# Attention and a max-of-three FFN on one core: scores as stationary operand, per-partition normalization, paired heads, and an instruction order written by hand

## The chip, the cores and the metric

The kernel runs on one core of one Trainium2 chip. The metric is the device time of a whole execution in microseconds (us). A kernel's executions mostly agree within 1.5%; where one fell in a slower state it is left out of the medians and the ratios, and this is said. "Span" is the time from the first to the last instruction in the trace; the timed value of the same execution is some 2 us longer (261.6 against 259.6 us). Engines: PE is TensorE (PEld its weight loads), DVE VectorE, ACT ScalarE, POOL GpSimd, SP SyncE.

## The reference

```python
# q, k, v: (4 batches, 8 heads, 768 positions, 64), fp32; n_sink = 4, window = 64
rel    = pos[:, None] - pos[None, :]
causal = rel >= 0
keep   = causal & ((pos[None, :] < n_sink) | (rel < window))   # streaming heads
mask   = causal for heads with is_retrieval == 1, keep for the others
a   = softmax(where(mask, q @ k.T / 8, -1e9))
x   = (a @ v), heads side by side          # (3072 tokens, 512)
h   = maximum(maximum(x @ w1, x @ w2), x @ w3)      # d_ff = 768
out = h @ w_out                            # (3072, 512), fp32
```

Which heads are retrieval heads is data. So each kernel computes the whole causal triangle for all heads. Near the diagonal it multiplies the exponentials by a mask; for keys two blocks or more back it uses a copy of V scaled by the head's flag (`vf`; `va` is V with a column of ones, which yields the softmax sums).

## The kernel before

Both kernels work on pairs of heads, 16 pairs in all, four to a batch. The parts that the change touches:

```python
# loads: cast to fp16 by DMAs that POOL issues, one batch at a time
nc.gpsimd.dma_start(out=qn, in_=q[b].rearrange("h (sb p) d -> p h sb d", p=P))   # kn, vn alike
# prep of a pair: 24 transposes, one per head and block, for q and k; vf by VectorE
nc.tensor.transpose(tqv[hl*D:(hl+1)*D, sb*P:(sb+1)*P], qn[:, 2*hp+hl, sb, :], ident)
nc.vector.tensor_scalar(out=vf[:, 1:NSB, hl, 0:D+1], in0=va[:, 1:NSB, hl, 0:D+1],
                        scalar1=RT[:, h:h+1], scalar2=None, op0=ALU.mult)
# ... scores, exp, and a mask of 256 columns per head and key block on POOL ...
# value product: V is the stationary operand, the scores stream; out is [65, queries]
nc.tensor.matmul(op_t[0:D+1, a0:a1], lhs,                      # lhs: va or vf
                 pt[:, ki, a0-ki*P : a1-ki*P], start=..., stop=...)
nc.vector.tensor_copy(out=osg[0:D+1, 0:S], in_=op_t[0:D+1, 0:S])
nc.sync.dma_start(out=sdram[h:h+1, 0:S], in_=osg[D:D+1, 0:S])  # the sums go to DRAM
# ... at the batch's end, all eight heads:
nc.sync.dma_start(out=sums_b[0:H, 0:S], in_=sdram)
nc.vector.reciprocal(out=rcp[0:H, 0:S], in_=sums_b[0:H, 0:S])
nc.sync.dma_start(out=rdram, in_=rcp[0:H, 0:S])
for h in range(H):
    nc.sync.dma_start(out=bc[0:D, 0:S], in_=rdram[h:h+1, 0:S].to_broadcast([D, S]))
    nc.vector.tensor_tensor(out=xTb[hp][hb:hb+D, 0:S], in0=ostages[h][0:D, 0:S],
                            in1=bc[0:D, 0:S], op=ALU.mult)
# order: the FFN of batch b is written whole, after the attention of batch b+1
if pending_ffn is not None:
    ffn_batch(*pending_ffn)
pending_ffn = (xTb, b * S)
```

A scheduler then orders the instructions on each engine.

The softmax here doesn't subtract the row's maximum and nothing guards it: scores larger than these inputs give would overflow.

Of the kernel before, what the change touches and what calls it, by code (L numbers as in the profile page):

```python
# [9 lines left out]
FP16 = mybir.dt.float16  # L10
# [4 lines left out]
NEG = -30000.0  # L15


def _split_at(a, b, cut):
    out = []
    if a < min(b, cut):  # L20
        out.append((a, min(b, cut)))
    if max(a, cut) < b:
        out.append((max(a, cut), b))
    return out
# [3 lines left out]
def kernel(  # L28
# [14 lines left out]
    nc = tc.nc  # L43
# [6 lines left out]
    HD = H * D  # L50
    KS = HD // P
# [4 lines left out]

    assert D == 64, "kernel assumes head_dim == 64"
    assert S % P == 0 and HD % P == 0 and DF % P == 0 and NT % P == 0
    assert window <= P and n_sink <= P
    assert DMdl <= 512, "final matmul free dim must fit one PSUM bank"  # L60

    consts = ctx.enter_context(tc.tile_pool(name="consts", bufs=1))
    persist = ctx.enter_context(tc.tile_pool(name="persist", bufs=1))
    qkvp = ctx.enter_context(tc.tile_pool(name="qkvp", bufs=2))
    pairp = ctx.enter_context(tc.tile_pool(name="pairp", bufs=3))
    headp = ctx.enter_context(tc.tile_pool(name="headp", bufs=4))
    ostp = ctx.enter_context(tc.tile_pool(name="ostp", bufs=H + 2))
    bcp = ctx.enter_context(tc.tile_pool(name="bcp", bufs=2))
    bcp3 = ctx.enter_context(tc.tile_pool(name="bcp3", bufs=3))
    xtp = ctx.enter_context(tc.tile_pool(name="xtp", bufs=2))  # L70
    htp = ctx.enter_context(tc.tile_pool(name="htp", bufs=2))
    ptp = ctx.enter_context(tc.tile_pool(name="ptp", bufs=3))
    fwork = ctx.enter_context(tc.tile_pool(name="fwork", bufs=3))
    sps = ctx.enter_context(tc.tile_pool(name="sps", bufs=4, space=bass.MemoryType.PSUM))
    ops = ctx.enter_context(tc.tile_pool(name="ops", bufs=1, space=bass.MemoryType.PSUM))
    fsp = ctx.enter_context(tc.tile_pool(name="fsp", bufs=2, space=bass.MemoryType.PSUM))
    dramp = ctx.enter_context(tc.tile_pool(name="dramp", bufs=2, space=bass.MemoryType.DRAM))

    ident = consts.tile([P, P], FP16, name="ident")
    make_identity(nc, ident)  # L80

    tri = consts.tile([P, P], FP16, name="tri")
    nc.gpsimd.memset(tri, 0.0)
    nc.gpsimd.affine_select(
        out=tri, in_=tri, compare_op=ALU.is_ge, fill=NEG,
        base=0, pattern=[[1, P]], channel_multiplier=-1,
    )
    ediagn = consts.tile([P, P], FP16, name="ediagn")
    nc.gpsimd.memset(ediagn, 0.0)
    nc.gpsimd.affine_select(  # L90
        out=ediagn, in_=ediagn, compare_op=ALU.is_gt, fill=NEG,
        base=window, pattern=[[-1, P]], channel_multiplier=1,
    )
    ediag0 = consts.tile([P, P], FP16, name="ediag0")
    nc.vector.tensor_copy(out=ediag0, in_=ediagn)
    if n_sink > 0:
        nc.vector.memset(ediag0[0:n_sink, :], 0.0)
    esubn = consts.tile([P, P], FP16, name="esubn")
    nc.gpsimd.memset(esubn, 0.0)
    nc.gpsimd.affine_select(  # L100
        out=esubn, in_=esubn, compare_op=ALU.is_gt, fill=NEG,
        base=-window, pattern=[[-1, P]], channel_multiplier=1,
    )
    esub0 = consts.tile([P, P], FP16, name="esub0")
    nc.vector.tensor_copy(out=esub0, in_=esubn)
    if n_sink > 0:
        nc.vector.memset(esub0[0:n_sink, :], 0.0)
    tri01 = consts.tile([P, P], FP16, name="tri01")
    nc.gpsimd.memset(tri01, 1.0)
    nc.gpsimd.affine_select(  # L110
        out=tri01, in_=tri01, compare_op=ALU.is_ge, fill=0.0,
        base=0, pattern=[[1, P]], channel_multiplier=-1,
    )
    w01dn = consts.tile([P, P], FP16, name="w01dn")
    nc.vector.tensor_copy(out=w01dn, in_=tri01)
    nc.gpsimd.affine_select(
        out=w01dn, in_=w01dn, compare_op=ALU.is_gt, fill=0.0,
        base=window, pattern=[[-1, P]], channel_multiplier=1,
    )
    w01d0 = consts.tile([P, P], FP16, name="w01d0")  # L120
    nc.vector.tensor_copy(out=w01d0, in_=w01dn)
    if n_sink > 0:
        nc.vector.tensor_copy(out=w01d0[0:n_sink, :], in_=tri01[0:n_sink, :])
    w01sn = consts.tile([P, P], FP16, name="w01sn")
    nc.gpsimd.memset(w01sn, 1.0)
    nc.gpsimd.affine_select(
        out=w01sn, in_=w01sn, compare_op=ALU.is_gt, fill=0.0,
        base=-window, pattern=[[-1, P]], channel_multiplier=1,
    )
    w01s0 = consts.tile([P, P], FP16, name="w01s0")  # L130
    nc.vector.tensor_copy(out=w01s0, in_=w01sn)
    if n_sink > 0:
        nc.vector.memset(w01s0[0:n_sink, :], 1.0)
    cause01 = consts.tile([P, 2 * P], FP16, name="cause01")
    nc.vector.tensor_copy(out=cause01[:, 0:P], in_=tri01)
    nc.vector.memset(cause01[:, P : 2 * P], 1.0)
    wmc_n = consts.tile([P, 2 * P], FP16, name="wmc_n")
    nc.vector.tensor_copy(out=wmc_n[:, 0:P], in_=w01dn)
    nc.vector.tensor_copy(out=wmc_n[:, P : 2 * P], in_=w01sn)
    nc.vector.tensor_tensor(out=wmc_n, in0=wmc_n, in1=cause01, op=ALU.subtract)  # L140
    wmc_0 = consts.tile([P, 2 * P], FP16, name="wmc_0")
    nc.vector.tensor_copy(out=wmc_0[:, 0:P], in_=w01d0)
    nc.vector.tensor_copy(out=wmc_0[:, P : 2 * P], in_=w01s0)
    nc.vector.tensor_tensor(out=wmc_0, in0=wmc_0, in1=cause01, op=ALU.subtract)
# [5 lines left out]
    )  # L150
    retr_row = consts.tile([P, H], FP32, name="retr_row")
# [3 lines left out]
    RB = consts.tile([P, H], FP32, name="RB")  # L155
    nc.vector.tensor_scalar(
        out=RB[:, 0:H], in0=RT[:, 0:H], scalar1=-1.0, scalar2=1.0,
        op0=ALU.mult, op1=ALU.add,
    )
    sinkcol = consts.tile([P, 1], FP32, name="sinkcol")  # L160
    nc.vector.memset(sinkcol, 0.0)
    if n_sink > 0:
        nc.vector.memset(sinkcol[0:n_sink, :], 1.0)
    rowfac = consts.tile([P, H], FP32, name="rowfac")
    for h in range(H):
        nc.vector.tensor_tensor(
            out=rowfac[:, h : h + 1], in0=RT[:, h : h + 1],
            in1=sinkcol[:, 0:1], op=ALU.max,
        )

    w_t = [persist.tile([P, KS, DF], FP16, name=f"w{wi}t") for wi in range(3)]
    woutt = persist.tile([P, NNB, DMdl], FP16, name="woutt")
# [8 lines left out]
    TBW = next(w for w in (384, 512, 256, 128) if S % w == 0)  # L181

    def ffn_batch(xTb, t_glob):
        hTb = [htp.tile([P, S], FP16, tag=f"hT{i}", name=f"hT{i}") for i in range(NNB)]
        for tb0 in range(0, S, TBW):
            for ni in range(NNB):
                acc = fwork.tile([P, TBW], FP32, tag="facc")
                for wi, wt in enumerate(w_t):
                    yy = fsp.tile([P, 512], FP32, tag="fsp", name="yy")
                    for ks_i in range(KS):  # L190
                        nc.tensor.matmul(  # L191
                            yy[:, 0:TBW],
                            wt[:, ks_i, ni * P : (ni + 1) * P],
                            xTb[ks_i][:, tb0 : tb0 + TBW],
                            start=(ks_i == 0), stop=(ks_i == KS - 1),
                        )
                    if wi == 0:
                        nc.scalar.copy(out=acc, in_=yy[:, 0:TBW])  # L198
                    elif wi == 1:
                        nc.vector.tensor_tensor(  # L200
                            out=acc, in0=acc, in1=yy[:, 0:TBW], op=ALU.max
                        )
                    else:
                        nc.vector.tensor_tensor(  # L204
                            out=hTb[ni][:, tb0 : tb0 + TBW],
                            in0=acc, in1=yy[:, 0:TBW], op=ALU.max,
                        )
        for tb0 in range(0, S, P):
            yo = fsp.tile([P, 512], FP32, tag="fsp", name="yo")
            for ns in range(NNB):  # L210
                nc.tensor.matmul(  # L211
                    yo[:, 0:DMdl],
                    hTb[ns][:, tb0 : tb0 + P],
                    woutt[:, ns, 0:DMdl],
                    start=(ns == 0), stop=(ns == NNB - 1),
                )
            ot = fwork.tile([P, DMdl], FP32, tag="ot")
            nc.scalar.copy(out=ot, in_=yo[:, 0:DMdl])
            nc.sync.dma_start(out=out[t_glob + tb0 : t_glob + tb0 + P, :], in_=ot)
# [199 lines left out]
```

## Time and profile before

| | before |
|---|---|
| time, median of 4 runs beside the changed kernel | 359.1 us |
| span of the profiled run | 355.8 us |
| start / attention alone / attention and FFN / FFN alone | 27 / 85 / 205 / 39 us |

The first lines of the profile's page give busy time, share of the span and instructions of each engine:

```profile
PE 281.7 (79%) x1776; PEld 152.1 (43%) x1776; DVE 228.8 (64%) x417; ACT 131.4 (37%) x329; POOL 163.2 (46%) x226
```

PE's 79% looks like a bound, but the durations of its matmuls overlap; the prediction works out from spacings that its work is about 198 us. The timeline of VectorE at the end of the first batch's attention (start, us, line, operation, count) shows why the FFN starts late:

```profile
88.24 4.93 DVE L364 RECIPROCAL rcp<-sums_b 8x768 f32<-8x768 f32 x1
...
103.07 0.94 DVE L373 TENSOR_TENSOR xT<-osg,bc 64x768 f16<-64x768 f32 x1
103.94 5.39 DVE L269 TENSOR_SCALAR vf<-va,RT 128x325 f16<-128x325 f16 x1
104.58 4.75 DVE L358 COPY osg<-op_t 65x768 f32<-65x768 f32 x1
```

The sums are there at 88 us. Between the reciprocal and the first product lie 10 us, with a store, a broadcast load and preparation of other pairs; after it VectorE stands 5 us in a `vf` and an `osg` whose normal durations are 0.3 and 0.95 us. The first FFN matmul is at 112.2 us.

### The profile page before, as it was taken

The page shows a single profiled execution, that of the slowest core. Times are in us where ns is not written, and L with a number is a line of the kernel's source. Part 1 is how long each engine was busy: PE and PEld are TensorE (multiplying, and loading weights), DVE is VectorE, ACT ScalarE, POOL GpSimd, SP SyncE. Part 2 cuts the span into 40 slices and gives each one's busy share as a digit, 9 for nine tenths or more (in the row PEclk, how much of TensorE's full clock was granted, in tenths as well). Part 3 has the DMA queues.
Part 4 walks back from the last instruction along what each step waited for, and adds up shares of the span by engine and source line. Part 5 has one row for each costly group of instructions (what it writes and reads, how often), then busy time and mean ns, then how long its engine had stood idle before and what let it go on. Part 6 is the DMA issues. An engine that isn't in the chain of part 4 may idle for free.

```text
span 355.8 us, 4977 instructions
## 1 busy us (share of the span) xinstructions
PE 281.7 (79%) x1776; PEld 152.1 (43%) x1776; DVE 228.8 (64%) x417; ACT 131.4 (37%) x329; POOL 163.2 (46%) x226
## 2 busy tenths in 40 slices
PE   0028698668886869997998896979979859899995
PEld 0013365344455435553544453435445534445542
DVE  2715475479789988999935877983454485915530
ACT  1006426605642613426255420704756311132223
POOL 3550999949978952527327700731557400000000
PEclk9999999955576978999999998989999996999999
DMA  0999999999999990032040001201300003240004
GB/s 0 79 150 192 199 91 89 85 69 77 93 135 130 136 88 6 0 92 92 21 158 1 3 3 57 102 22 59 120 2 3 1 5 92 88 177 2 0 5 173
DMA packets 82522, 25.78 MB, mean 72 GB/s; under 512 B 74978, under 2 KB 77282, under 8 KB 82498
## 3 DMA queue, kind: packets, MB, share of 16 engines
q0 software_dynamic: 76288, 12.58, 50.9%
q1 hardware_dynamic: 6210, 12.88, 11.0%
q8 instruction: 14, 0.23, 0.3%
q14 instruction: 10, 0.08, 0.1%
HBM read 31.56 MB, written 6.49 MB: 107 GB/s over the span
## 4 chain that ended last, share of the span: by engine, by line
PE 35%; DVE 15%; POOL 9%; issue 5%; ACT 2%; DMA 1%; POOLq 0%; DVEq 0%; ACTq 0%
PE yy L191 19%; POOL pt L322 9%; PE yo L211 8%; DVE xT L373 4%; PE op_t L349 4%; PE st L307 2%; DVE acc L200 2%; DVE osg L358 2%; ACT pt L315 2%; DVE rcp L364 2%; DVE hT L204 1%; DVE vf L269 1%; DMA bc<-rdram 1%; DVE va L264 1%; DVE dm_n L278 1%
## 5 line engine op out<-in xcount | busy, mean ns | idle before, releaser
L315 ACT ACTIVATE pt<-st 128x512 f16<-128x512 f32 (+3 forms) x256 | 94.9, 473 | 105.5 <-PE st L307 99.4
L322 POOL TENSOR_TENSOR pt<-pt,dm_n 128x256 f16<-128x256 f16 (+1 forms) x160 | 106.3, 695 | 21.6 <-DVE va L267 11.0
L307 PE MATMUL st<-QT,KT 64*128 64x512 f16 (+3 forms) x256 | 56.5, 348 | 15.1 <-ACT pt L315 9.3
L322 POOL TENSOR_TENSOR pt<-pt,dm 128x256 f16<-128x256 f16 x32 | 23.9, 761 | 80.4 <-ACT pt L315 70.3
L349 PE MATMUL op_t<-pt,va 128*65 128x256 f16 (+1 forms) x224 | 50.2, 281 | 13.2 <-POOL pt L322 7.7
L198 ACT COPY acc<-yy 128x384 f32<-128x384 f32 x48 | 23.1, 480 | 91.0 <-PE yy L191 88.3
L191 PE MATMUL yy<-xT,w0t 128*128 128x384 f16 x192 | 44.4, 346 | 15.2 <-DVE acc L200 13.2
L358 DVE COPY osg<-op_t 65x768 f32<-65x768 f32 x32 | 34.1, 1066 | 26.6 <-PE op_t L349 26.5
L200 DVE TENSOR_TENSOR acc<-acc,yy 128x384 f32<-128x384 f32 x48 | 26.1, 544 | 33.3 <-PE yy L191 33.2
L191 PE MATMUL yy<-xT,w1t 128*128 128x384 f16 x192 | 44.0, 343 | 2.6 <-ACT acc L198 2.3
L191 PE MATMUL yy<-xT,w2t 128*128 128x384 f16 x192 | 41.6, 339 | 0.0
L349 PE MATMUL op_t<-pt,vf 128*65 128x256 f16 x192 | 41.4, 290 | 0.0
L307 PEld LDWEIGHTS <-KT 64*128 64x128 f16 x256 | 15.8, 97 | 50.4 <-issue 38.4
L245 PE MATMUL tq<-ident,qn 128*64 128x128 f16 x192 | 21.0, 261 | 19.5 <-DMA qn<-in_q_dram 19.4
L373 DVE TENSOR_TENSOR xT<-osg,bc 64x768 f16<-64x768 f32 x32 | 35.0, 1095 | 0.8 <-DMA bc<-rdram 0.2
L349 PEld LDWEIGHTS <-va 128*65 128x65 f16 x224 | 25.4, 125 | 18.7 <-issue 12.3
L191 PEld LDWEIGHTS <-w0t 128*128 128x128 f16 x192 | 18.6, 101 | 32.6 <-issue 24.5
L211 PE MATMUL yo<-woutt,hT 128*128 128x512 f16 x144 | 31.9, 379 | 0.2
L204 DVE TENSOR_TENSOR hT<-acc,yy 128x384 f16<-128x384 f32 x48 | 26.3, 549 | 3.7 <-PE yy L191 1.4
L278 DVE SCALAR_TENSOR_TENSOR dm_n<-wmc_n,RB,cause 128x256 f16<-128x256 f16 x32 | 17.8, 563 | 16.1 <-POOL pt L322 16.1
L349 PEld LDWEIGHTS <-vf 128*65 128x65 f16 x192 | 22.2, 126 | 12.1 <-issue 9.4
L191 PEld LDWEIGHTS <-w1t 128*128 128x128 f16 x192 | 18.4, 101 | 19.4 <-issue 9.9
(62 smaller groups left out, 256.6 us busy)
## 6 DMA issues: line engine op xcount, KB each, us to landing
bc<-rdram SPq DMA_DIRECT2D x32, 192.0 KB
out_dram<-ot SPq DMA_DIRECT2D x24, 256.0 KB
qn<-in_q_dram POOLq DMA_DIRECT2D x4, 768.0 KB, 9.5
kn<-in_k_dram POOLq DMA_DIRECT2D x4, 768.0 KB, 9.4
vn<-in_v_dram POOLq DMA_DIRECT2D x4, 768.0 KB, 9.9
w0t<-in_moe_w_dram POOLq DMA_DIRECT2D x1, 768.0 KB, 11.5
w1t<-in_moe_w_dram POOLq DMA_DIRECT2D x1, 768.0 KB, 14.9
w2t<-in_moe_w_dram POOLq DMA_DIRECT2D x1, 768.0 KB, 17.9
```

Source lines behind the costliest of these rows:

```text
L191: nc.tensor.matmul(yy[:, 0:TBW], wt[:, ks_i, ni * P : (ni + 1) * P], xTb[ks_i][:, tb0 : tb0 + TBW], start=(ks_i == 0), stop=(ks_i == KS - 1),)
L198: nc.scalar.copy(out=acc, in_=yy[:, 0:TBW])
L200: nc.vector.tensor_tensor(out=acc, in0=acc, in1=yy[:, 0:TBW], op=ALU.max)
L204: nc.vector.tensor_tensor(out=hTb[ni][:, tb0 : tb0 + TBW], in0=acc, in1=yy[:, 0:TBW], op=ALU.max,)
L211: nc.tensor.matmul(yo[:, 0:DMdl], hTb[ns][:, tb0 : tb0 + P], woutt[:, ns, 0:DMdl], start=(ns == 0), stop=(ns == NNB - 1),)
L278: nc.vector.scalar_tensor_tensor(out=dm_n, in0=wmc_n, scalar=RB[:, h : h + 1], in1=cause01, op0=ALU.mult, op1=ALU.add,)
L307: nc.tensor.matmul(st[:, 0 : c1 - c0], KT[hb : hb + D, q0 : q0 + P], QT[hb : hb + D, q0 + c0 : q0 + c1], start=True, stop=True,)
L315: nc.scalar.activation(out=pts[hl][:, ki, c0:c1], in_=sts[hl][:, 0 : c1 - c0], func=AF.Exp, scale=sc,)
L322: nc.gpsimd.tensor_tensor(out=pts[hl][:, ki, 0:dmw], in0=pts[hl][:, ki, 0:dmw], in1=dm[:, 0:dmw], op=ALU.mult,)
L349: nc.tensor.matmul(op_t[0 : D + 1, a0:a1], lhs, pt[:, ki, a0 - ki * P : a1 - ki * P], start=(idx == 0 or bank_of[idx - 1] != bk), stop=(id ...
L358: nc.vector.tensor_copy(out=osg[0 : D + 1, 0:S], in_=op_t[0 : D + 1, 0:S])
L373: nc.vector.tensor_tensor(out=xTb[hp][hb : hb + D, 0:S], in0=ostages[h][0:D, 0:S], in1=bc[0:D, 0:S], op=ALU.mult,)
```

## The change

The intent is to give each query its own partition, so that the division by the sum is a per-partition product and the sums never leave the core, and to mix the FFN of a finished batch finely into the attention of the next. The core of the diff (cut; the constants, the pools and the score tiles also change):

```diff
-  nc.gpsimd.dma_start(out=qn, in_=q[b]...)            # whole batches, cast by the DMA
+  nc.sync.dma_start(out=s, in_=src[b, 2*hp:2*hp+2]...)  # fp32, one pair at a time, five pairs ahead
+  nc.vector.tensor_copy(out=qn, in_=qs.rearrange("p h sb d -> p sb h d"))   # kn and va alike
-  nc.vector.tensor_scalar(out=vf[...], in0=va[...], scalar1=RT[:, h:h+1], ...)
+  nc.gpsimd.tensor_scalar(out=vf[...], in0=va[...], scalar1=RT[:, h:h+1], ...)
+  # one transpose, one exp and one mask instruction serve both heads of a pair
+  nc.tensor.transpose(tr[:, sb*P:(sb+1)*P], src[:, sb].rearrange("p h d -> p (h d)"), ident)
   nc.tensor.matmul(
-      op_t[0:D+1, a0:a1], lhs, pt[:, ki, a0-ki*P : a1-ki*P],
+      o[:, qi, hl, 0:D+1], pt[:, u, hl, c:c+P], vv[:, 2*hp+hl, ki, 0:D+1],
-  # sums to DRAM, reciprocal, broadcast from DRAM, product (as shown above)
+  nc.vector.reciprocal(out=rc, in_=o[:, :, :, D])
+  nc.vector.tensor_tensor(out=x, in0=o[:, :, :, 0:D],
+                          in1=rc.unsqueeze(3).to_broadcast([P, 3, 2, D]), op=ALU.mult)
+  # x is then transposed (three blocks of two heads) and copied into xT
+  ctx.enter_context(tc.manual_schedule())             # engines keep the order written
+  for i in range(NP + 1):                             # pairs, p = i - 1
+      if i + 1 < NP: qn, kn = prep(i + 1)             # casts and vf of the next pair
+      for u in range(6):
+          scores(i, u, *cur)                          # scores, exp, masks of pair i
+          # value product, normalization, transposes of pair p, spread over the units
+          fill(RATE)                                  # 2 of the 48 pieces of a batch's FFN
+      if i + 5 < NP: load(i + 5)
+      if i == 0: load_weights()
```

## The prediction

> **What bounds the kernel now.** I read the page first, for which engine is full when; then the windows view, one row per stage; then the timeline of the matmuls, for what one really costs; then the groups of instructions. The page's slices (8.9 us each, busy share in tenths):
>
> ```profile
> PE   0028698668886869997998896979979859899995
> ...
> DVE  2715475479789988999935877983454485915530
> ...
> POOL 3550999949978952527327700731557400000000
> PEclk9999999955576978999999998989999996999999
> ```
>
> In slices 4 to 9 (36 to 90 us) POOL is at 9 and PE at 5 to 8, with the granted clock halved from 71 us: attention alone is bound by POOL's mask multiplies. From slice 14 on (125 us) POOL falls to 2 to 7 and PE is mostly at 9: the FFN has joined. The windows view puts lengths on it (columns: us, then busy us and count of each engine, granted clock, DMA):
>
> ```profile
> 27.00:112.00 85.00, 66.28 (x412) 38.26 (x408) 59.01 (x112) 39.38 (x108) 68.89 (x87) 0.80 1.37 116
> 112.00:127.00 15.00, 12.69 (x110) 7.89 (x107) 14.81 (x20) 7.50 (x21) 13.71 (x14) 0.90 1.04 109
> 127.00:187.00 60.00, 53.64 (x341) 28.29 (x341) 50.30 (x97) 24.07 (x58) 22.96 (x33) 0.94 0.36 67
> 187.00:247.00 60.00, 50.94 (x338) 26.97 (x336) 44.78 (x73) 21.89 (x56) 24.24 (x35) 0.94 0.09 29
> 317.00:356.00 39.00, 34.60 (x183) 17.43 (x181) 13.30 (x24) 9.86 (x19) 0.00 (x0) 0.98 0.15 56
> ```
>
> So: 27 us of start (the first score matmul is at 26.57), 85 us with no FFN matmul at all (the first is at 112.2), 205 us mixed (112 to 317), 39 us of the last batch's FFN alone. In the first of these POOL is busy 68.9 of 85 us; in the mixed part PE is "busy" 85 to 89% of it, but those durations overlap. The timeline gives true spacing:
>
> ```profile
> 268.18 0.52 PE L245 MATMUL tq<-ident,qn 128*64 128x128 f16 x6
> 270.71 0.50 PE L307 MATMUL st<-QT,KT 64*128 64x512 f16 x4
> 328.52 0.81 PE L191 MATMUL yy<-xT,w0t 128*128 128x384 f16 x4
> 330.70 0.81 PE L191 MATMUL yy<-xT,w0t 128*128 128x384 f16 x4
> 343.80 7.93 PE L211 MATMUL yo<-woutt,hT 128*128 128x512 f16 x36
> ```
>
> Four 384-column matmuls take 0.81 us of which one is 0.32 (the shortest in the tile view): (0.81-0.32)/3 = 163 ns each, 0.425 ns per column. 36 of 512 columns: 7.93/36 = 220 ns. Six transposes: (0.52-0.22)/5 = 60 ns. The four score matmuls (two heads x 512, two heads x 256) end after 0.50 us, where one after the other they would need 0.65 plus a latency: the two heads run at the same time. A value product of one head (13 matmuls, 2688 columns) is 1.17 us in the chain of waits.
>
> PE work per head pair, from these: FFN share 36 x 163 + 9 x 220 = 7.8 us; scores 2688 x 0.425 = 1.15; 24 transposes some 1.1; value products 2 x 1.17 = 2.35. Sum 12.4 us, x16 = 198 us of 356. **PE is therefore not the bound of the whole**: the loss is 112 us before the FFN starts and a mixed part that takes 205 us for work worth about 150.
>
> **What the Trainium skill says.** (1) "TensorE: Matmul & The Clock Gate", Weight-path perf modes: fast weight load is on when there are 128 weights and the type is not fp32. The trace agrees in tendency: a load of 128 columns is 101 ns, of 65 columns 125 ns on average. This matters because scores become weights. (2) Same page, Part 3 (row/col tiling): small matmuls in different row groups run together; the 0.50 us above agrees. (3) "SBUF — State Buffer", Who interferes with whom: a VectorE copy in a two-port mode and a GpSimd operation exclude each other for a whole instruction. The trace agrees: vf (325 elements, VectorE) takes 309 ns at best, 5393 at worst. (4) "VectorE: DVE Perf Modes", the perf-mode tier table: an fp32 SBUF copy reaches 2x. No row of this trace shows one.
>
> **The change, part by part.** The rows that price it:
>
> ```profile
> L322 POOL TENSOR_TENSOR pt<-pt,dm_n 128x256 f16<-128x256 f16 x128 | 92.2, 748 | 21.6 <-DVE va L267 11.0 <-ACT pt L315 9.7 <-DVE osg L358 0.5
> L315 ACT ACTIVATE pt<-st 128x512 f16<-128x512 f32 x96 | 55.0, 612 | 93.4 <-PE st L307 87.8 <-PE op_t L349 5.5
> L373 DVE TENSOR_TENSOR xT<-osg,bc 64x768 f16<-64x768 f32 x32 | 35.0, 1095 | 0.8 <-DMA bc<-rdram 0.2
> L358 DVE COPY osg<-op_t 65x768 f32<-65x768 f32 x32 | 34.1, 1066 | 26.6 <-PE op_t L349 26.5
> L204 DVE TENSOR_TENSOR hT<-acc,yy 128x384 f16<-128x384 f32 x48 | 26.3, 549 | 3.7 <-PE yy L191 1.4
> L364 DVE RECIPROCAL rcp<-sums_b 8x768 f32<-8x768 f32 x4 | 19.7, 4932 | 0.0
> ```
>
> *Normalization.* osg, rcp and xT go, 88.8 us of VectorE, and with them the way of the sums through DRAM, the chain at each batch's end (rcp, store, broadcast, eight multiplies) that holds back the FFN. In their place per pair and half: one reciprocal of 6 elements (est. 0.2 us), one product of 384 elements from PSUM (0.55, as hT), one copy of 384 fp16 (est. 0.35, from 0.546 for 768). 1.1 x 2 x 16 = 35 us.
>
> *Value product.* 42 matmuls of 65 columns per pair replace 26 of up to 256. Streamed columns halve (2730 for 5376, 1.15 us), but each needs a load of 128 columns. I estimate 55 ns each, the smallest spacing that weight load plus 128-column matmul show here: 2.3 us per pair, no gain. Transposes: 12 for q and k (two heads in one) plus 6 for x, 18 x 56 = 1.0 us. **PE per pair 12.3 us: unchanged.** The gain must come from order.
>
> *Loads.* q, k, v come as fp32 by SP: POOL loses 27.7 us of issue (12 x 2.3), VectorE gains three copies of 768 fp32 per pair (est. 0.48 each from the tier table, 23 us in all) that exclude POOL.
>
> *Masks.* 2816 elements per pair as before, in 6 instructions for 12. From 657 ns (256) and 415 (128): 1.89 ns per element plus 0.17: 6.3 us per pair. vf moves to POOL (est. 1.5). **POOL 7.8 us per pair**, some 9 with the exclusions.
>
> *ACT.* 6 wide exps for 16; slope 0.79 ns per element ((612-310)/384), so 5.5 us per pair and 2.3 of FFN copies: 8, not a bound. VectorE: 1.45 casts, 1.1 QT and KT, 2.2 normalization, 3.3 FFN: 8 us plus waits for POOL.
>
> *Order.* Pairs 0 to 3 run without FFN, then each pair's six units each take 2 of the 48 FFN pieces of a batch, so exactly one batch of FFN per four pairs; the last batch's FFN stays alone.
>
> Stages: (a) start: 24 mask-building instructions at 0.395 us spacing after RT (9.4 us in the trace) reach 19 us, then casts and transposes: first scores at 22 us (before 26.6). (b) 4.3 pairs at POOL's 8.8 us: 38. (c) 12 pairs at PE's 12.3 plus about 1.1 for waits that the bufs=1 accumulators and the start of a pair (three casts ahead of the FFN evictions) leave: 13.4 x 12 = 161. (d) tail: 38, as before. Sum 259 us of span; the timed value is 3.3 us over the span (359.1 against 355.8): **262 us**, 27% less.
>
> **The rivals.** *The weight load binds*: at 100 ns per value matmul a pair grows by 1.9 us, 12 x 1.9 = 23 us, to 285. For it: loads last 97 to 125 ns in the trace. Against: they overlap, and 128-column matmuls with their loads follow at 55 to 60 ns. *VectorE or its exclusion with POOL becomes the bound*: if each cast waits out POOL's 1024-element mask (est. 2.1 us), VectorE reaches 13 us per pair, PE waits for FFN evictions with only two banks, and a pair takes 15 to 16 us: 285 to 295. For it: the 5393 ns above. Against: casts are early in a pair and POOL has 5 us idle in each. *The loads bind stage (b)*: fp32 pairs are 1.18 MB; at 8.8 us that is 134 GB/s, and the trace shows up to 210 in 10 us, beside weights of 6.3 MB. If not, plus 10 us. *The fixed order is worse than the scheduler's*: in-order engines with single buffers for oacc and tr could stall PE at each unit; with 0.5 us a unit, 36 us more, to 298. It would take all of these to reach 359.
>
> **Range and chances.** Best case (8 us and 12.4 us per pair) gives 22+34+149+37+3 = 245; one rival in full gives 285 to 295. Range 245 to 288. Faster by over 2%: 0.96; within: 0.02; slower: 0.02.
>
> **What would show it.** Right: first FFN matmul near 60 us; mixed part near 13.4 us per pair with PE full; POOL full only before it; value matmuls near 55 ns apart; VectorE near 150 us in all. Wrong: value matmuls near 100 ns; casts of over 1.5 us and FFN matmuls waiting for VectorE; PE waiting for loads; a mixed part over 15 us per pair.

## The result

The changed kernel is correct and takes 262.5 us (median of 4 runs, 261.4 to 264.6) against 359.1 us of the kernel before. Ratios here are the mean time of one kernel's fast runs over that of the other's of the same rounds, so not quite the ratio of the quoted medians: 0.734, with a 95% interval of 0.728 to 0.740. That is 27% less.

The page of the changed kernel, span 259.6 us in slices of 6.5 us:

```profile
PE   0004675785699999999999999999999999999993
...
POOL 2006999997997777777677868595959552000000
```

From slice 11 on (71 us) PE is at 9 in all slices but the last, where before it stood at 5 to 9. POOL is at 9 only in slices 4 to 11, and there in all but one. The windows view by stage, with the columns of the prediction's windows:

```profile
22.40:71.00 48.60, 32.57 (x313) 18.69 (x313) 30.51 (x44) 24.21 (x27) 47.13 (x49) 1.00 1.23 210
71.00:223.00 152.00, 151.71 (x1480) 83.16 (x1478) 96.50 (x200) 87.96 (x124) 107.66 (x116) 1.00 0.37 81
223.00:260.00 37.00, 32.39 (x173) 16.41 (x171) 13.62 (x25) 8.77 (x17) 0.00 (x0) 1.00 0.12 43
```

| stage | before | predicted | after |
|---|---|---|---|
| start, to the first scores | 27 | 22 | 22.4 (first scores at 23.8) |
| attention alone | 85 | 38 | 48.6 |
| attention and FFN | 205 | 161 | 152 |
| FFN alone | 39 | 38 | 37 |

The windows were cut at 22.4 us; by the first score matmul, as in the other two columns, the first two stages are 23.8 and 47.1 us.

Of the 96 us of span that went, 53 came out of the mixed part and 36 out of the stage before it. These groups answer to the rows that priced the change (form; busy us in all, mean ns; idle before):

```profile
L284 POOL TENSOR_TENSOR pt<-pt,mk 128x512 f16<-128x512 f16 (+2 forms) x96 | 103.3, 1100 | 23.1 <-ACT pt L280 23.0
L240 POOL TENSOR_SCALAR vf<-va,RT 128x325 f16<-128x325 f16 x32 | 35.5, 1108 | 29.3 <-DVE va L238 27.9
L234 DVE CAST qn<-qs 128x768 f16<-128x768 f32 x16 | 21.0, 1315 | 0.1
L324 DVE TENSOR_TENSOR x<-oacc,rc 128x384 f16<-128x384 f32 x32 | 17.8, 557 | 1.1
```

The product by the reciprocals costs 17.8 us of VectorE in all; `osg`, `xT` and `rcp` had cost 88.8. One scaling of `vf` on POOL takes 1108 ns, and a cast 1315 ns on average, though the shortest takes 549. The chain of waits (start, us, what) in the mixed part:

```profile
83.14 0.57 PE oacc L309 x15
83.71 0.17 PE tr L337 x3
83.88 1.30 PE yy L187 x8
85.18 0.27 PE st L273 x2
```

Here each step follows on PE itself, nothing waits: fifteen value matmuls take 0.57 us to the end of the last. In the stage before, the same view shows another picture:

```profile
28.84 7.13 POOL pt L284 x6
...
42.21 4.37 DVE qn L234
...
47.52 0.94 DVE va L238
...
48.60 0.57 DVE x L324
49.21 1.14 PE oacc L309 x15
```

The six masks of a pair, then a cast that lasts 4.37 us instead of some 0.5 beside POOL's masks (in maskdve below, with no masks on POOL, the longest cast of q takes 0.78 us), then two more casts, and only then the normalization for which PE waits. VectorE runs them in the order in which they are written.

### The profile page after: what moved, and what is told of

It reads as the page before. It is cut to its first block, busy times and chain, and to the rows that moved or that the text cites. A ratio compares the mean times of both kernels' runs of the same rounds, so it can differ in the third digit from the quotient of the medians.

```text
span 259.6 us, 4937 instructions
## 1 busy us (share of the span) xinstructions
PE 217.5 (84%) x1968; PEld 119.0 (46%) x1968; DVE 153.5 (59%) x305; ACT 122.2 (47%) x169; POOL 157.3 (61%) x174
## 4 chain that ended last, share of the span: by engine, by line
PE 69%; DVE 10%; POOL 9%; SPq 5%; DMA 2%; issue 2%; ACT 0%; DVEq 0%; ACTq 0%; POOLq 0%
PE yy L187 34%; PE yo L205 12%; PE oacc L309 9%; PE st L273 7%; POOL pt L284 5%; SPq L103 5%; PE tr L253 4%; DVE qn L234 3%; PE tr L337 3%; POOL vf L240 3%; DMA qs<-in_q_dram 2%; DVE kn L235 2%; DVE va L238 2%; POOL vf L244 1%; DVE acc L198 1%
## 5 line engine op out<-in xcount | busy, mean ns | idle before, releaser
L280 ACT ACTIVATE pt<-st 128x1024 f16<-128x1024 f32 (+1 forms) x96 | 87.4, 919 | 69.9 <-PE st L273 67.1
L284 POOL TENSOR_TENSOR pt<-pt,mk 128x512 f16<-128x512 f16 (+2 forms) x96 | 103.3, 1100 | 23.1 <-ACT pt L280 23.0
L240 POOL TENSOR_SCALAR vf<-va,RT 128x325 f16<-128x325 f16 x32 | 35.5, 1108 | 29.3 <-DVE va L238 27.9
L198 DVE TENSOR_TENSOR acc<-yy,acc 128x384 f16<-128x384 f32 x48 | 26.8, 558 | 37.9 <-PE yy L187 33.2
L195 ACT CAST acc<-yy 128x384 f16<-128x384 f32 x48 | 23.0, 478 | 44.7 <-PE yy L187 44.7
L273 PE MATMUL st<-QT,KT 64*128 64x384 f16 (+2 forms) x288 | 39.3, 330 | 4.5 <-DVE KT L258 3.3
L309 PEld LDWEIGHTS <-pt 128*128 128x128 f16 x672 | 27.3, 103 | 26.9 <-issue 10.6
L309 PE MATMUL oacc<-va,pt 128*128 128x65 f16 x352 | 32.1, 203 | 5.6 <-POOL pt L284 5.5
L309 PE MATMUL oacc<-vf,pt 128*128 128x65 f16 x320 | 26.9, 204 | 5.0 <-DVE x L324 5.0
L198 DVE TENSOR_TENSOR hT<-yy,acc 128x384 f16<-128x384 f32 x48 | 26.6, 554 | 3.7 <-PE yy L187 0.6
L234 DVE CAST qn<-qs 128x768 f16<-128x768 f32 x16 | 21.0, 1315 | 0.1
```

Of the source, the lines that this page charges most:

```text
L195: nc.scalar.copy(out=acc, in_=yy[:, 0:HALF])
L198: nc.vector.tensor_tensor(out=dst, in0=yy[:, 0:HALF], in1=acc, op=ALU.max)
L234: nc.vector.tensor_copy(out=qn, in_=qs.rearrange("p h sb d -> p sb h d"))
L240: nc.gpsimd.tensor_scalar(out=vf[j][:, h, 1:NSB, 0 : D + 1], in0=va[j][:, h, 1:NSB, 0 : D + 1], scalar1=RT[:, h : h + 1], scalar2=None, op ...
L273: nc.tensor.matmul(st[:, hl, c0 : c0 + n], KT[hb : hb + D, ki * P : (ki + 1) * P], QT[hb : hb + D, q0 : q0 + n], start=True, stop=True,)
L280: nc.scalar.activation(out=pt[:, u, :, 0:width], in_=st[:, :, 0:width], func=AF.Exp, scale=sc)
```

## The experiments

The kernel before had medians of 356.9 to 359.4 us. All gave correct results. Every ratio is to the kernel before. The first eight have the changed kernel's 262.5 us for comparison, which a later run of the changed kernel on the chip of these eight confirms:

**base**: the changed kernel again.

> The changed kernel as it is, run again on the chip of the next two so that they have something to be compared with: 260 to 265 us, 0.73 to 0.74 of the kernel before. It tests no theory.

Measured: 262.6 us, ratio 0.731 (0.726 to 0.736). One thing differs. Its attention-only window is

```profile
22.40:71.30 48.90, 31.01 (x312) 18.39 (x312) 31.57 (x45) 24.35 (x27) 47.43 (x49) 0.78 1.22 209
```

with a granted clock of 0.78, where the first profile had 1.00 for the same work in the same time. Six transposes last up to 0.83 us there in both, against 0.50 us in the mixed part. So the 1.00 of the first profile is not to be believed in that stage: PE ran slower there in both.

### Parts of the change, alone and undone

**normalone**: the kernel before, with only the new value product and normalization.

```diff
-  op_t[0:D+1, a0:a1], lhs, pt[...]              # then osg, sums through DRAM, bc, xT
+  o[:, qi, 0:D+1], pt[:, ki, (qi-ki)*P:(qi-ki+1)*P], vv[:, ki, hl, 0:D+1]
+  reciprocal of o[..., D], product, six transposes of two heads, one copy into xT
```

The run also gives the accumulator two PSUM buffers where both kernels have one; so does ordernorm below.

> One part of the change alone, in the kernel before: scores as the stationary operand of the value product, normalization per partition, transposes of x; no sums through DRAM, no broadcast. Loads, masks, exps, FFN and the scheduler stay as before. Theory (the way through DRAM holds the FFN back and loads VectorE with 89 us, so it is a large part of the 97 us): first FFN matmul at about 95 us for 112, mixed part 205 down to 180: 310 to 330 us. Rival (POOL's masks and the order are what counts, the normalization was hidden): 350 to 359 us.

Measured: 355.4 us, ratio 0.995 (0.990 to 1.000). VectorE's busy time fell from 228.8 to 169.6 us, and the first finished FFN block comes at 91.8 us instead of 130.0; the time did not follow. The FFN is still written whole behind the next batch's attention: 306 of its 720 matmuls run after the last value matmul (320 in the kernel before, 186 in ordernorm below). So an earlier start of the FFN alone is worth nothing here.

**orderonly**: the kernel before, its normalization through DRAM kept, the FFN in 48 pieces among the attention of the next batch.

```diff
+                    yield                        # after each FFN piece
+            fill(1)                              # after each score chunk, fill(2) after each head
-        if pending_ffn is not None: ffn_batch(*pending_ffn)
+        queue.append(ffn_batch(xTb, b * S))
```

> The kernel before with its normalization through DRAM kept, and only the FFN written in 48 pieces between the steps of the next batch's attention. Theory (both parts are needed: the chain of sums, reciprocal, broadcast and eight multiplies at each batch's end delays the first pieces, and on an in-order engine what comes behind them): less than half of the gain, 310 to 345 us. Rival (the order alone is the gain): 265 to 290 us.

Measured: 384.9 us, ratio 1.077 (1.071 to 1.083): 8% slower than the kernel before, well outside what I expected. The timeline at the last batch shows the cause:

```profile
324.86 4.94 DVE L378 RECIPROCAL rcp<-sums_b 8x768 f32<-8x768 f32 x1 [3.43 <-DMA sums_b<-sdram]
...
334.82 2.91 DVE L387 TENSOR_TENSOR xT<-osg,bc 64x768 f16<-64x768 f32 x3 [5.02 <-DMA bc<-rdram]
...
336.81 0.50 PE L191 MATMUL yy<-xT,w0t 128*128 128x384 f16 x1 [15.07 <-DVE xT L387]
```

Late FFN pieces used to fill the time in which the sums travel through DRAM. With the FFN used up among the attention (186 matmuls left after the last value matmul, not 320), PE stands 15 us there, and 22.5 us in all, in waits for `xT`, where the kernel before has 1.7 us of them. The last batch's FFN then takes 48 us instead of 39 (337 to 385 us), at a granted clock of 0.85 instead of 0.98.

**ordernorm**: both of these together.

> The kernel before with two parts of the change: the new value product and normalization (as in the run that had it alone), and the FFN written in 48 pieces per batch between the steps of the next batch's attention. Loads, masks, single-head exps and the scheduler stay as before. Theory (the overlap is the gain and the new normalization is what makes it possible): 27 us of start, 4 pairs at 10 us, 12 pairs at 13 to 14, 38 of tail: 265 to 290 us. Rival (fewer, wider instructions and loads off POOL are needed as well): over 310 us.

Measured: 305.3 us, ratio 0.853 (0.848 to 0.858), between the two expectations. The two parts that gain nothing alone (2 us, and a loss of 27) gain 52 us together, more than half of the change's 97. About 43 us are left for the loads, the wider instructions and the order.

**sched**: the changed kernel without its line that keeps the written order.

```diff
-    ctx.enter_context(tc.manual_schedule())
```

> The changed kernel with its fixed engine order undone: the line that asks for the program's own order is taken out and the scheduler places the instructions, as in the kernel before. Theory A (the order as written gives the gain; a scheduler brings back waits as in the kernel before, some 15 to 16 us per mixed pair): 285 to 310 us. Theory B (the program is already written interleaved, and the scheduler starts from that; what counts is which work exists): 255 to 270 us, perhaps a little better at the start, because it moves the first casts ahead of the 24 mask instructions.

Measured: 270.7 us, ratio 0.758 (0.754 to 0.762). The mixed part keeps its pace (80 to 231 us, 151 us); the first FFN block that is complete (all three products) comes only at 81 us. So the hand-written order is worth 8 us, all of it before the FFN, and the other 35 of the 43 us are loads, wider instructions and the emission order that the scheduler starts from; no run splits these three.

**block**: the changed kernel with a batch's FFN in one piece.

```diff
-            fill(RATE)
+            if u == 5 and p >= 0 and p % NHP == NHP - 1:
+                while queue: fill(1)
```

> The changed kernel with one thing undone: the FFN of a batch is not spread over the six units of four pairs, but runs in one piece at the end of the pair after the batch. Theory (the gain is the overlap: FFN pieces fill PE while POOL and ACT make the next masks): pairs go back to POOL's 10 to 11 us without FFN, and each FFN block takes 31 to 34 us: per batch 4 x 10.4 + 33 = 75 us for 50.6, three times: +73 us, 330 to 340 us. Rival (PE's work is a fixed sum and the order matters little): within 5% of the changed kernel, 255 to 275 us.

Measured: 320.0 us, ratio 0.894 (0.889 to 0.899): 57 us more, where I had expected about 70 or more. The slices show the two kinds of work take turns:

```profile
PE   0035837679999977779999978769999878799995
...
POOL 2039999899000389997000489996000889400000
```

Of the parts that a run takes out of the changed kernel, the fine mix is the largest (57 us; the written order 8). The estimate was too high because attention alone was cheaper per pair here than I had assumed: four pairs between two FFN blocks take 34 to 35 us, 8.5 to 8.8 us each for 10.4.

### The value product

**av2**: every value matmul issued twice into the same sum (numerator and denominator double, so the result stays right).

```diff
+            for rep in range(2):
                 nc.tensor.matmul(o[:, qi, hl, 0:D+1], pt[:, u, hl, c:c+P], ...,
-                    start=(idx == 0), stop=(idx == len(todo) - 1))
+                    start=(idx == 0 and rep == 0), stop=(idx == len(todo) - 1 and rep == 1))
```

> Every value matmul of the changed kernel is issued twice (numerator and row sum both double, so the result stays right). This measures what one value matmul with its 128-column weight load costs on the path. Theory (from the profile after: 15 of them take 0.57 us with a latency of 0.20, so 27 to 32 ns each; in the mixed part PE has no gap): 12 pairs x 42 x 32 ns = 16 us in the mixed part, and about nothing in the first 71 us, which POOL bounds: 277 to 282 us. Rival, the figure of the prediction (55 ns): 12 x 42 x 55 = 28 us, 290 us. Rival, the weight load shows in full (100 ns): over 310 us.

Measured: 277.4 us, 276.3 to 278.5 in three runs, ratio 0.776 (0.771 to 0.781). The fourth, profiled execution took 574.6 us. Against base it is 14.8 us more (by the ratios 16, give or take 2.5) for 12 x 42 = 504 additional matmuls in the mixed part: **about 30 ns each**, each with its own load of 128 columns, if those of the first four pairs cost nothing. The trace of the changed kernel agrees: in its mixed part fifteen value matmuls take 0.48 us from the first one's start to the start of what follows, 32 ns each. The prediction's 55 ns and its rival of 100 ns are both out.

### The stage of attention alone

**maskdve**: the masks on VectorE instead of POOL.

```diff
-            nc.gpsimd.tensor_tensor(
+            nc.vector.tensor_tensor(
                 out=pt[:, u, :, c0:c0+n], in0=pt[:, u, :, c0:c0+n], in1=mk[...], op=ALU.mult)
```

> The changed kernel with one cost moved: the six mask multiplies of a pair run on VectorE (16-bit, both inputs in SBUF), not on POOL, which keeps vf alone. It asks what bounds the first 71 us. Theory POOL (masks 7.1 and vf 3.1 us per pair are the bound): masks cost VectorE some 2 to 3 us per pair, a pair falls from 10.2 to about 8 us, first FFN matmul at 55 to 62 us, mixed part unchanged (VectorE 8.3 + 2.5 of 12.6): 247 to 255 us. Rival DMA (the queue moves 210 to 218 GB/s without a break until 66 us): first FFN matmul stays at 68 to 71 us, 259 to 265 us in all. Rival VectorE: mixed pairs grow beyond 13.5 us and eat the gain: over 262.

Measured: 270.1 us, ratio 0.756 (0.752 to 0.760), 8 us slower. Its two windows, attention alone and mixed:

```profile
22.40:68.50 46.10, 31.54 (x313) 18.73 (x311) 31.26 (x73) 24.06 (x27) 23.02 (x28) 0.87 1.22 213
68.50:230.00 161.50, 151.89 (x1455) 82.13 (x1453) 112.46 (x264) 87.78 (x123) 33.76 (x40) 0.99 0.36 77
```

POOL is busy half of the first window instead of all of it, and the window is 2.5 us shorter. So POOL's fullness was not what set this stage's length by itself; but the run puts the masks onto VectorE, which is in the other chain of this stage, so it does not remove POOL's work cleanly (vfact below comes closer). The mixed part loses 9.5 us, 13.5 us a pair, as the rival VectorE had it: the normalization now queues behind the masks, and PE waits 8.1 us there for the accumulator that it frees, and 0.2 us for FFN evictions.

**prepfirst**: the 24 mask-building instructions moved behind the first pair's casts and transposes.

> The changed kernel with the 24 mask-building instructions on VectorE moved behind the casts and transposes of the first pair. Theory DMA (the first pair's loads land only at about 20 us, as the chain of waits says for qs): no gain, 261 to 264 us. Rival (the 9.5 us of mask building hold the first scores): first scores 6 to 9 us earlier, but POOL still needs the masks at 20 to 22 us, so the first masks come at 28 us as before and the gain is 0 to 3 us: 259 to 262.

Measured: 265.7 us, ratio 0.743 (0.738 to 0.747), no gain, though the first scores come at 13.4 us instead of 23.8. The first cast ran at 9.7 us, so its load had long landed and the chain's "DMA qs" step at the start is not what held it. But POOL's first `vf` then lasted from 16.45 to 25.26 us, beside mask building on VectorE, and the first masks came at 31.1 us instead of 28.8.

**vfact**: the scaling of `vf` on ACT, in unit 4 of the pair.

```diff
-            nc.gpsimd.tensor_scalar(out=vf[...], in0=va[...], scalar1=RT[:, h:h+1], ...)
+            nc.scalar.activation(out=vf[...], in_=va[...], func=AF.Copy, scale=RT[:, h:h+1])
```

> The scaling of the far values (vf) moves from POOL to ACT, late in the pair; everything else as in the changed kernel. POOL loses 3.15 us of each pair, ACT gains about 1.5 to 2. Theory A (in the attention-only stage POOL's work sets the pace, 10.3 us a pair, of which vf was the mis-sized 3.15): the stage shortens to 7.5 to 8.5 us a pair, the first FFN matmul comes at 59 to 63 us instead of 70.9, the time falls by 8 to 12 us. Theory B (POOL is only one of several chains of the same length: the run with the masks on VectorE kept its 10.4 us a pair although POOL was free): the first FFN matmul stays at 67 or later and the time falls by less than 4 us. In both the mixed pairs stay at 12.65 us, because PE sets them.

Measured: 259.5 us, three runs 257.7 to 260.3, ratio 0.723 (0.717 to 0.728). By the ratios that is 3 us less than base, give or take 2.7: theory A's 8 to 12 us are out, theory B's "less than 4" is likely. The profiled execution fell in the slow state (521.2 us), so its stages are no measure of the fast ones; but even in it, with slower matmuls, the first FFN matmul came at 65.9 us (71.4 in base), earlier than theory B allows. So `vf` probably did hold the stage somewhat; no fast profile shows it.

**vfactw**: also the weights issued by POOL at its start.

```diff
+    load_weights()
     qn, kn = prep(0)
...
-        if i == 0: load_weights()
```

> As the run before, and POOL issues the four weight transfers at its start, before the first pair, instead of after it (3.4 us of POOL's time in the attention-only stage). Theory A: another 2 to 4 us earlier than the run before, unless the loads of pairs 1 to 4 come late behind 6.3 MB of weights; then the stage is bound by the queue: 4.7 MB and 6.3 MB at 200 to 218 GB/s need 50 to 55 us, so the first FFN matmul cannot come before about 60 us. Theory B: no change, within 2 us.

Measured: 255.6 us, ratio 0.715 (0.709 to 0.722); first FFN matmul at 64.0 us. Against vfact that is 3.8 us less by the medians and 2.6 by the ratios, give or take 3, so this step alone is not clear of the noise; the two steps together gain 5.6 us on base by the ratios, give or take 2.8, which is. Neither theory is decided. POOL is now busy 28.7 of 43 us in the stage (21 to 64 us). The chain there:

```profile
16.24 18.60 DMA vs<-in_v_dram
...
34.87 1.63 DVE va L238
...
36.63 0.57 DVE x L328
...
37.25 1.00 PE oacc L313 x15
```

The casts of pair 2 stand in VectorE's order ahead of the normalization of pair 0, and wait for k and v from DRAM, behind the weights; the finished accumulator of pair 0 waits with them, and PE waits for the one accumulator buffer: 4.9 us here, 6.3 us in the stage.

**spread**: vfactw with the three casts taken apart.

```diff
+                if u == 1: prep_k(i + 1, kn)      # behind the first half's normalization
+                elif u == 4: prep_v(i + 1)        # behind the second half's
```

> The last run once more (vf on ACT, weights issued early), and the three casts of the next pair no longer stand in one block ahead of the normalization on VectorE: the cast of k follows the first half's normalization, that of v comes in unit 4. In the last run VectorE, in order, waited at 32 to 36 us for k and v of pair 2 from DRAM while the finished accumulator of pair 0 stood before the normalization and PE waited for it (6.4 us there, about 1.5 us in each later pair of the stage). Theory (that in-order wait is what the stage lost once POOL was free): first FFN matmul at 56 to 60 us instead of 63.9, time 248 to 252 us. Rival (transfers bind the stage: about 11 MB at 210 GB/s have to be in by then): first FFN matmul stays at 62 or later, time within 2 us of 255.6.

Measured: 247.3 us, five runs 246.9 to 250.3; one slow run of 251.9 is left out, and so are three of the kernel before (359.0 to 361.3); ratio 0.699 (0.693 to 0.705). The windows of the stage and of the mixed part:

```profile
20.00:58.00 38.00, 28.95 (x321) 17.89 (x322) 24.65 (x48) 28.91 (x43) 29.24 (x26) 0.91 1.17 214
58.00:210.00 152.00, 152.00 (x1487) 83.55 (x1486) 92.01 (x203) 103.21 (x174) 77.31 (x71) 1.00 0.47 99
```

The theory holds and the rival falls: the transfers run at 214 GB/s as before and did not keep the first FFN matmul from coming at 57.5 us. PE's waits for the accumulator fell from 6.3 to 1.0 us in the stage. The mixed part is unchanged at 152 us. This version beats both kernels; it was timed against the kernel before in its own rounds (0.699), not directly against the changed kernel (0.731). It was run on another chip.

## Why the prediction was right or wrong

- **The total** (262.0 for 262.5 us; its last step adds 3.3 us from two different executions, where one execution shows 2.0, so the sum was 261) was right, and so was the claim that the gain comes from order and not from less PE work. normalone shows that the arithmetic alone gains nothing; block shows that without the mix 57 us are gone. That the two parts need each other was said only implicitly: orderonly and ordernorm show it (385 and 305 us). Its reading of the kernel before was too simple in three places: "the loss is 112 us before the FFN starts", but in normalone the FFN finishes its first block 38 us earlier for nothing; POOL is not at 9 in all of slices 4 to 9 (slice 8, where the clock is halved, reads 4), and that its masks bound attention alone there no run tests; and 24 transposes at its own 60 ns are 1.44 us, not 1.1.
- **Start, tail, VectorE**: right. First scores at 23.8 us (22, a little late), FFN alone 37 us (38), VectorE busy 153.5 us (near 150), fp32 casts of 549 ns at the shortest (0.48).
- **Mixed part, 13.4 us a pair**: 152 us for 12 pairs, 12.65 each. The step that failed is "I estimate 55 ns each, the smallest spacing that weight load plus 128-column matmul show here". That spacing belongs to 128 streamed columns; a value matmul streams 65. av2 and the trace give 30 to 32 ns, 1.3 us a pair for 2.3. The Trainium skill, page "TensorE: Matmul & The Clock Gate", section Back-to-back issue gap, has a warm spacing of N/2.4 + 2.5 ns, by which I estimate 29.6 ns for 65 columns, and says that this under-counts at small N; here it does so by some 2 ns. With 1.3 the sum of PE work is 11.3 us. The remaining 1.4 us lie for the most part around the score matmuls, as the timeline of PE shows:

```profile
84.36 0.81 PE L187 MATMUL yy<-xT,w1t 128*128 128x384 f16 x4
85.11 0.34 PE L273 MATMUL st<-QT,KT 64*128 64x384 f16 x2
85.38 0.20 PE L309 MATMUL oacc<-vf,pt 128*128 128x65 f16 x1
```

The four FFN matmuls are through at 85.01 us by their 163 ns of spacing, the two score matmuls start at 85.11, together (both end after 0.34 us), and the next value matmul starts at 85.38: 0.37 us for 384 columns, which need 0.16. The groups of two and of four score matmuls in the mixed part (69) all take some 0.2 us more than their columns; six such groups make about 1.2 us a pair. Around them the weight loads do not run ahead: those of these scores start at 85.11 us, with their matmuls, where those of FFN matmuls start 0.16 us before. What holds them no run isolates. The 1.1 us that were allowed for waits were not needed: PE is busy 151.7 of 152.0 us.
- **Attention alone, "4.3 pairs at POOL's 8.8"**: 47.1 us for 38. Two things were wrong. First the size: `vf` "est. 1.5" measured 2 x (1108 + 473) ns = 3.2 us a pair (I priced it like a mask, per element), and the four weight issues on POOL (3.4 us) were not counted. Second, the mechanism was incomplete: maskdve freed POOL and kept the stage at 46 us, and vfact took 3.2 us a pair off POOL for a gain of some 3 us in all. Beside POOL's chain stands one of nearly the same length, from PE through VectorE in order and back through one accumulator buffer, at a PE clock of 0.78; spread shortens that one: with the same work on POOL as in vfactw, the first FFN matmul comes at 57.5 us instead of 64.0.
- The two errors, +9 us in attention alone and -9 us in the mixed part, cancelled, as did +1.8 us at the start and -1 us in the tail. The range held because the rivals were sized, but the centre was partly luck.
- **The rivals**: the weight load does not bind (30 to 32 ns). The exclusion of VectorE and POOL is real (the cast of q takes up to 4451 ns, at most 780 ns where POOL has no masks, and a `vf` takes 8.8 us in prepfirst), but costs time only before the FFN; in the mixed part PE never waits for it. The loads do not bind as a whole: the queue is full at some 210 GB/s until about 72 us, yet spread brings the FFN forward 13 us. In vfactw they did hold VectorE, by 3.8 us (3.0 for k, 0.8 for v). The fixed order is better than the scheduler's, by 8 us.

What stays open: how the 35 us between ordernorm and sched divide among loads, wider instructions and written order, what exactly costs the time around the score matmuls, and how much of the first stage's gain is `vf` and how much the weights. Nor is it shown what bounds that stage in spread: its queue is still full (221 GB/s from 66 to 70 us).

## What to carry to other kernels

Removing work from an engine off the path gains nothing until the order lets the bound engine use the time; try the two together before either is given up. On an engine that runs in order, put what another engine waits for (the normalization that frees an accumulator) ahead of what only prepares (casts that wait for a load). Price a matmul by its own streamed columns, and an elementwise instruction by a row of the same operation on the same engine, or count it as unknown.

## What the Trainium skill lacked or had wrong

- "TensorE: Matmul & The Clock Gate", Back-to-back issue gap: it says that streams of load and matmul sustain about 81 ns at 128 columns and that the isolated formula under-counts at small N. Here 65-column matmuls, each with its own 128-column fp16 load, follow at 30 to 32 ns (504 of them cost some 15 us; fifteen take 0.48 us), close to the isolated formula, and six 128-column transposes with their loads take 0.34 us, 56 ns each.
- The same page, Part 3 (row/col tiling), tells the gain from several row groups, but not the cost of changing between these and full-height matmuls; "TensorEngine Tiling (Array Packing)", Key Properties, says that a change of tiling mode drains TensorE, and no page gives the time. A group of two score matmuls amid others took 0.37 us for 0.16 us of columns; that the drain is the cause is not shown.
- The same page, Seeing it yourself, warns that the records of clock changes can be unreliable. The runs show how far the granted clock can be off: 1.00 and 0.78 for the same stage of the same kernel at equal length, and two executions of 574.6 and 521.2 us with a recorded clock of 1.00, in the second of which a 384-column FFN matmul lasted 732 ns instead of 326. The duration of a known matmul form is the better gauge.
- "GPSIMD Engine Reference", 3.1 Elementwise: it gives two-input work as the dearer per element. Here the one-input scaling by a per-partition factor cost (1108 - 473) / 260 = 2.4 ns per element and the two-input mask (2141 - 706) / 768 = 1.9 ns, both in fp16. For one-input work, 4.1 of the same page says only that it is roughly line-rate; no page gives this form's cost.
